# w_out's sums and low halves on GpSimd, x's copies on ScalarE, conversion stages asked for engine by engine

## The chip, the cores and the metric

One core of one Trainium2 chip. The time is that of one execution on the device, in microseconds (us). The five engines each work through their own instructions in order: TensorE (PE in the profile; PEld its weight loads), VectorE (DVE), ScalarE (ACT), GpSimd (POOL) and SyncE (SP), which here asks for nearly all DMAs.

## What is computed

```python
scores = scale * x @ state^T;  xread = softmax(scores) @ state          # x: 8 x 8 heads x 512 x 64
scores2 = scale * state @ x^T; sread = softmax(scores2) @ x             # state: 8 x 8 x 32 x 64
x1 = concat([xread, sread], axis=2), heads side by side                 # 8 x 544 rows of 512
a = x1 @ w1; b = x1 @ w2; x2 = ((a * b) @ w3) @ w_out                   # 512 -> 1024 -> 1024 -> 512
a = x2 @ w_a; b = x2 @ w_b; out = (a * b) @ w_out2                      # 512 -> 1536 -> 512
```

The inputs are doubles. The kernel takes them in as pairs of 32-bit words, and multiplies with matrices that are split into a high and a low half: three products (high by high, high by low, low by high) stand for one.

## The kernel before, in words

**Stages.** First, a list of jobs (`run_jobs`) converts w1, w2, w3 and the first w_out, does the attention of blocks 0 and 1 in part and layer 0; it ends at about 150 us. Then come the layers of attention blocks 1 to 6, one after the other, and at last the layer of block 7 interleaved with the small layer of the state rows (`one` and `one_s`): this is the first block, to about 530 us. The second block (`block2`) takes the eight batches in four pairs g = 0 to 3 and runs to the end; in g = 0 it also computes the state rows.

**A layer.** A layer has eight steps f (`step`, called from `block1`). In a step TensorE makes `ap`, ScalarE copies it to `asbp`, TensorE makes `bp`, VectorE multiplies the two into `hfp` (L1188), and `split` makes the high half on ScalarE (L149) and the low half on VectorE (L155). Only then does TensorE accumulate the step before into four PSUM banks (`flush`, L1223). So four of the eight banks hold the layer's sums, and the other four go around among `ap`, `bp` and whatever attention work needs one.

**What is filled in.** `fills1` has two calls in a step: `middle`, after `ap`, and `behind`, after the split. Each places attention work of the following blocks by the tables MIDDLE and BEHIND and then lets the planner place conversion stages. In step 6 x of block b + 2 is transposed by TensorE (its half 0, two banks), and the banks are copied out behind that step by `x_move`; step 7 does the same with half 1. Each even step also splits a piece of p: ScalarE makes `ph`, GpSimd `pl`; the loads of p are asked for three pieces ahead.

**The conversions.** Three `Intake` objects take in weights that are needed later: `sw` (w1 and w2 again, for the state layer), `ab` (w_a and w_b) and `iz` (the second w_out, class `IntakeZ`). A task is a list of stages: two takes on ScalarE, a join on VectorE (`make`, L199), sums and differences of quarters, high halves on ScalarE with low halves on VectorE or GpSimd, and stores to DRAM. `ab`'s even columns have their sums on GpSimd and low halves on VectorE, the odd ones the other way round; `sw`'s columns have low halves on the one or the other. For w_out all sums (L1113) and all low halves were on VectorE. Here and below w_out, without more, is this second one. One of its tasks covers one of six column blocks c: parts `za`, `zb`, `zc`, `zd`, each stored to `z_d` from SP. The first read of `z_d` is in the second half of g = 0 in `block2`.

**The planner.** `now` is a clock that the kernel's writer advances by an estimate of TensorE's work, `through[e]` when engine e (A ScalarE, V VectorE, G GpSimd, D the DMA queues) is expected to be through with what was asked of it, and `charge` adds a stage's cost to it. `Intake.run` asks for a task's next stages as long as none would begin later than `now` plus a horizon (1.5 in the layers for `sw` and `ab`, 2.0 there for `iz`; 1.5 in the state layer, 2.0 in the second block for all), and enough SBUF units are vacant. A stage that follows another is due 0.2, or 0.7 after a stage of several engines, after the end of that one. What is asked for goes into the engines' queues at that place. Nothing of this runs on the chip: it only fixes the order of instructions.

Of the kernel before, what the change touches and what calls it, by code (L numbers as in the profile page):

```python
# [15 lines left out]
ALU = mybir.AluOpType  # L16
# [42 lines left out]
SW_FROM = 46  # L59
LAG = 0.7  # L60
HORIZON = (1.5, 1.5, 2.0)
START_BY = 3.0
MARGIN = 1.5

# [8 lines left out]
def attention_moe_moe2(  # L73
# [17 lines left out]
    nc = tc.nc  # L91
    B, H, S, D = x.shape
# [24 lines left out]
    now = [0.0]  # L117
    through = {"A": 2.0, "V": 4.0, "G": 3.0, "D": 0.0}
# [21 lines left out]
    def room(n, by=None):  # L140
        return sum(by is None or t <= by for t, _ in vacant) >= n
# [265 lines left out]
    class Attention:  # L407
# [16 lines left out]

        def x_move(self, g):
            self.x_part(g, 0, "A")
            self.x_part(g, 1, "V")

        def x_part(self, g, j, e):
            (nc.scalar.copy if e == "A" else nc.vector.tensor_copy)(self.xt[g][:, j, :], self.banks.pop((g, j)))  # L430
# [153 lines left out]

    PE_COST = dict(x_transpose=0.9, scores=0.9, read=0.9, col_transpose=0.9)
    COST = dict(
        x_move=dict(A=0.6, V=0.7),
        scores_move=dict(A=0.7),
        maxima=dict(V=2.2),
        col_exp=dict(A=1.3),  # L590
# [3 lines left out]
        sums=dict(V=1.5),  # L594
# [268 lines left out]
    for n_early, name in enumerate(EARLY):  # L863
# [10 lines left out]
        elif name[:2] == "w3":  # L874
# [3 lines left out]
            for k in range(2):  # L878
# [13 lines left out]
                    need=2 - 2 * k,  # L892
# [65 lines left out]
    class Intake:  # L958
# [23 lines left out]
        def stages(self, f, raws):  # L982

            o = {}
            name = f"{self.name}{f}"
            eng = "GV"[f % 2]

            def take(i):
                if i == 0:
                    o["c"] = Convert(name, raws[:2])  # L990
                o["c"].take(i)

            def split_columns():
                hi, lo = unit(f"{name}h", F32R), unit(f"{name}l", F32R)
                split(hi, lo, o["c"].out, {"G": nc.gpsimd, "V": nc.vector}[eng])
                free(name)
                self.cols[f] = [v.rearrange("p (w k c) -> p w k c", k=4, w=2) for v in (hi, lo)]

            def halves(t):
                return t.rearrange("p (b c) -> p b c", b=4)  # L1000

            def sums():
                a11, a12, a21, a22 = (halves(o["c"].out)[:, i] for i in range(4))
                o["s"] = unit(f"{name}s")
                s1, s2, s3, s4 = (halves(o["s"])[:, i] for i in range(4))
                e = {"G": nc.gpsimd, "V": nc.vector}[eng]
                for out, x, y, op in (
                    (s1, a21, a22, ALU.add),
                    (s3, a11, a21, ALU.subtract),
                    (s2, s1, a11, ALU.subtract),  # L1010
                    (s4, a12, s2, ALU.subtract),
                ):
                    e.tensor_tensor(out=out, in0=x, in1=y, op=op)

            def split_part(i):
                src, part = ((o["c"].out, name), (o["s"], f"{name}s"))[i]
                hi, lo = (unit(f"w0_{f}_{2 * i + j}", F32R) for j in range(2))
                split(hi, lo, src, {"G": nc.gpsimd, "V": nc.vector}["VG"["GV".index(eng)]])
                free(part)
                o["p", i] = hi, lo  # L1020

            def store_part(i):
                for j, t in enumerate(o["p", i]):
                    for n in range(2):
                        a, b = PLACES[4 * i + 2 * n : 4 * i + 2 * n + 2]
                        nc.sync.dma_start(
                            out=w_d[f][:, a : b + 1 : b - a, j, :].bitcast(F32),
                            in_=t.rearrange("p (h b c) -> p h b c", h=2, b=2)[:, n].bitcast(F32),
                        )
                if f in AB_AT:  # L1030
                    free(*(f"w0_{f}_{2 * i + j}" for j in range(2)), at=until[0] + 2.5)
                else:
                    for m, t in enumerate(o["p", i]):
                        v = t.rearrange("p (b k c) -> p b k c", b=4, k=2)
                        for n in range(4):
                            w_t.setdefault((0, f, 4 * i + n), []).append(v[:, n])
                self.cols[f] = i == 1

            out = [
                (0, dict(A=1.1), lambda: take(0)),  # L1040
                (0, dict(A=1.1), lambda: take(1)),
                (1, dict(V=1.2), lambda: o["c"].make()),
            ]
            if self.plain:
                out.append((2, {"A": 1.1, eng: {"G": 2.4, "V": 1.1}[eng]}, split_columns))
            else:
                other = "VG"["GV".index(eng)]
                work = {"A": 1.1, other: {"G": 2.4, "V": 1.1}[other]}
                out += [
                    (1, {eng: {"G": 2.6, "V": 1.4}[eng]}, sums),  # L1050
                    (2, work, lambda: split_part(0)),
                    (0, dict(D=3.0), lambda: store_part(0)),
                    (2, work, lambda: split_part(1)),
                    (0, dict(D=3.0), lambda: store_part(1)),
                ]
            return deque(out)

        def run(self, horizon, force=False):
            for t in list(self.tasks):
                ready, stages = t  # L1060
                while stages:
                    need, work, go = stages[0]
                    begin = max(t[0], *(through[e] for e in work))
                    if not force and begin > now[0] + horizon:
                        break
                    if not room(need, None if force else now[0] + horizon + 1):
                        break
                    stages.popleft()
                    until[0] = t[0] = charge(**work) + (LAG if len(work) > 1 else 0.2)
                    go()  # L1070
                    until[0] = None
                if not stages:
                    self.tasks.remove(t)
# [13 lines left out]
    class IntakeZ(Intake):  # L1087
# [12 lines left out]
        def stages(self, c, raws):  # L1100
            o = {}

            def take(i):
                if i == 0:
                    o["c"] = Convert(f"z{c}", raws)
                o["c"].take(i)

            def sums():
                b11, b12, b21, b22 = (o["c"].out[:, i * 256 : (i + 1) * 256] for i in range(4))
                o["s"] = unit(f"zs{c}")  # L1110
                t2, t1, t3, t4 = (o["s"][:, i * 256 : (i + 1) * 256] for i in range(4))
                for out, x, y in ((t1, b12, b11), (t2, b22, t1), (t3, b22, b12), (t4, b21, t2)):
                    nc.vector.tensor_tensor(out=out, in0=x, in1=y, op=ALU.subtract)  # L1113

            def parts(name, src, terms):
                t = unit(name, F32R)
                v = t.rearrange("p (i q e) -> p i q e", i=2, q=2)
                src = src.rearrange("p (i e) -> p i e", e=256)
                n = len(terms)
                if n == 2 and src.shape[1] == 4:  # L1120
                    src = src[:, 0:4:2]
                split(v[:, :n, 0, :], v[:, :n, 1, :], src)
                for i, p in enumerate(terms):
                    nc.sync.dma_start(out=z_d[p][:, c].bitcast(F32), in_=v[:, i].bitcast(F32))
                free(name, at=until[0] + 3.0)

            def first():
                parts(f"za{c}", o["c"].out, (0, 1))

            def second():  # L1130
                parts(f"zb{c}", o["s"][:, :512], (2, 3))

            def third():
                parts(f"zc{c}", o["c"].out[:, 768:], (5,))
                free(f"z{c}")

            def fourth():
                parts(f"zd{c}", o["s"][:, 512:], (4, 6))
                free(f"zs{c}")
                self.cols[c] = True  # L1140

            work = dict(A=0.7, V=0.8, D=0.8)
            return deque(
                [
                    (0, dict(A=1.1), lambda: take(0)),
                    (0, dict(A=1.1), lambda: take(1)),
                    (1, dict(V=1.2), lambda: o["c"].make()),
                    (1, work, first),
                    (1, dict(V=1.6), sums),
                    (1, work, second),  # L1150
                    (1, work, third),
                    (1, work, fourth),
                ]
            )

    w_t = {}
    iz = IntakeZ("z", None, False, list(range(NF2 // 2)))
# [267 lines left out]
    for b, qs in ((0, range(4)), (1, range(3))):  # L1425
        for q in qs:
# [5 lines left out]
                need=1,  # L1432
# [83 lines left out]
    for b in range(B):  # L1516
# [9 lines left out]
        def fills1(f, b=b):  # L1526
            def middle():
                attend(MIDDLE, b, f)
                sw.run(HORIZON[0])
                ab.run(HORIZON[0])  # L1530
                iz.run(HORIZON[2])

            def behind():
                if f % 2 == 0:
# [24 lines left out]
                    ab.start(2, reserve=AB_RESERVE)  # L1559
                sw.run(HORIZON[0])  # L1560
                ab.run(HORIZON[0])
                iz.run(HORIZON[2])

            return middle, behind

# [446 lines left out]
```

## Time and profile before

| | us |
|---|---|
| runs, lowest / median / highest of 3 | 1313.37 / 1313.78 / 1316.99 |
| the profiled execution | 1314.6 |
| its span, first to last instruction | 1312.8 |
| TensorE busy | 1281.2 (98%) |
| VectorE busy | 735.3 (56%) |
| ScalarE busy | 569.6 (43%) |
| GpSimd busy | 497.6 (38%) |

The profile is of one execution. TensorE's busy time is a union of its matmuls' times, whose ends are modelled. A wait is idle time of an engine ahead of an instruction, put down to the engine that released it last.

### The profile page before, as it was taken

What the parts mean: (1) busy time and instruction counts of PE and PEld (TensorE: products, weight loads), DVE (VectorE), ACT (ScalarE), POOL (GpSimd) and SP (SyncE); (2) the same over time, 40 slices, a digit from 0 to 9 for tenths busy, and PEclk for the clock granted to TensorE, in tenths of its full rate; (3) what the DMA queues carried; (4) which work ended last, traced back from release to release, by engine and by line L of the source; (5) the groups of instructions that cost most, each with busy time, mean ns of one, the idle gap of its engine ahead of it and who ended that gap; (6) DMA issues with size and microseconds to landing.
All of it is one profiled execution on the core that took longest, in us unless ns stands there. A gap on an engine that the chain in (4) does not pass through costs nothing. (4 is left out here: it accounts for less than half of the span.)

```text
span 1312.8 us, 19793 instructions
## 1 busy us (share of the span) xinstructions
PE 1281.2 (98%) x7642; PEld 1082.0 (82%) x7642; DVE 735.3 (56%) x867; ACT 569.6 (43%) x932; POOL 497.6 (38%) x328
## 2 busy tenths in 40 slices
PE   7999999999999998999999999999999999999998
PEld 5666677877777887988889998889988889988898
DVE  6884145756665666565456862247922369433493
ACT  6876355655565665545233431123511235212232
POOL 3823124525334263345228341148311274212450
PEclk7999999999999999999999999999999999999999
DMA  9968765474556742789564769317695247873271
GB/s 328 346 191 263 230 213 192 129 240 134 199 182 193 237 167 70 264 283 306 196 226 144 248 238 389 127 27 250 203 404 200 64 162 263 331 275 107 81 256 65
DMA packets 129789, 276.55 MB, mean 211 GB/s; under 512 B 13600, under 2 KB 66848, under 8 KB 129696
## 3 DMA queue, kind: packets, MB, share of 16 engines
q1 hardware_dynamic: 125408, 260.09, 58.2%
q0 software_dynamic: 4288, 15.21, 2.9%
q8 instruction: 60, 0.98, 0.3%
q14 instruction: 33, 0.27, 0.1%
HBM read 205.00 MB, written 70.25 MB: 210 GB/s over the span
## 5 line engine op out<-in xcount | busy, mean ns | idle before, releaser
L1807 POOL TENSOR_TENSOR r<-e,e 128x512 f32<-128x512 f32 x48 | 64.2, 1337 | 305.6 <-DVE e L1632 305.6
L1223 PE MATMUL x2p<-hp,ws 128*128 128x512 f32 x672 | 162.2, 390 | 0.3 <-DVE hp L155 0.2
L155 POOL TENSOR_TENSOR pl<-pr,ph 128x512 fp32r<-128x512 f32 x64 | 85.9, 1362 | 174.4 <-ACT ph L149 115.7
L1223 PEld LDWEIGHTS x2p<-hp,ws 128*128 128x128 f32 x672 | 125.7, 188 | 26.9 <-DVE hp L155 0.5
L1752 ACT COPY e<-r 128x512 f32<-128x512 f32 x48 | 28.2, 588 | 190.0 <-PE r L1618 190.0
L1815 DVE TENSOR_TENSOR r<-e,r 128x512 f32<-128x512 f32 x48 | 32.9, 686 | 128.7 <-PE r L1618 128.7
L1188 DVE TENSOR_TENSOR hfp<-asbp,bp 128x512 f32<-128x512 f32 x56 | 38.2, 683 | 79.0 <-PE bp L1164 78.5
L1632 DVE TENSOR_TENSOR e<-e,q 128x512 f32<-128x512 f32 x48 | 32.9, 685 | 73.5 <-PE q L1618 73.3
L1656 POOL TENSOR_TENSOR r<-r,r 128x1024 f32<-128x1024 f32 x24 | 70.6, 2952 | 2.2 <-issue 1.2
L155 DVE TENSOR_TENSOR hp<-hfp,hp 128x512 fp32r<-128x512 f32 x56 | 46.5, 831 | 42.3 <-ACT hp L149 41.6
L1618 PE MATMUL r<-xT2h,w 128*128 128x512 f32 x192 | 67.2, 390 | 0.5 <-ACT e L1752 0.5
L1618 PE MATMUL r<-xT4h,w 128*128 128x512 f32 x192 | 67.1, 390 | 0.2 <-DVE e L1632 0.2
L1618 PE MATMUL r<-xT3h,w 128*128 128x512 f32 x192 | 67.2, 390 | 0.1
L1618 PE MATMUL r<-xB11h,w 128*128 128x512 f32 x192 | 67.0, 390 | 0.0
L1618 PE MATMUL v<-xT1h,w 128*128 128x512 f32 x192 | 66.9, 389 | 0.0
L1618 PE MATMUL q<-xB21h,w 128*128 128x512 f32 x192 | 66.9, 389 | 0.0
L1618 PE MATMUL v<-xB22h,w 128*128 128x512 f32 x192 | 66.9, 389 | 0.0
L149 ACT CAST hp<-hfp 128x512 fp32r<-128x512 f32 x56 | 34.7, 619 | 73.4 <-DVE hfp L1188 70.7
L1780 ACT COPY e<-r 128x512 f32<-128x512 f32 x48 | 28.3, 589 | 69.3 <-PE r L1618 69.3
L1182 ACT COPY asbp<-ap 128x512 f32<-128x512 f32 x56 | 32.8, 586 | 54.4 <-PE ap L1164 54.2
L1632 DVE TENSOR_TENSOR e<-e,v 128x512 f32<-128x512 f32 x48 | 32.8, 684 | 29.9 <-PE v L1618 22.6
L1164 PE MATMUL bp<-ah,ph 128*128 128x512 f32 x112 | 48.0, 429 | 0.0
(499 smaller groups left out, 3731.0 us busy)
## 6 DMA issues: line engine op xcount, KB each, us to landing
w<-w_d SPq DMA_DIRECT2D x132, 512.0 KB, 8.6
zz<-z_d SPq DMA_DIRECT2D x84, 512.0 KB, 4.3
w_d<-w SPq DMA_DIRECT2D x96, 256.0 KB, 5.0
p_d<-sg SPq DMA_DIRECT2D x128, 128.0 KB, 3.2
pr<-p_d SPq DMA_DIRECT2D x32, 512.0 KB, 5.7
w<-w_d SPq DMA_DIRECT2D x36, 256.0 KB, 8.8
x<-in_x_dram SPq DMA_DIRECT2D x16, 512.0 KB, 7.7
sw<-in_moe_w_dram SPq DMA_DIRECT2D x16, 512.0 KB, 5.6
```

The lines of the kernel that those rows point to most:

```text
L149: nc.scalar.copy(hi, src)
L155: (eng or nc.vector).tensor_tensor(out=lo[:, i], in0=src[:, i], in1=hi[:, i].bitcast(F32), op=ALU.subtract)
L1164: nc.tensor.matmul(dst[:, :n], lhsT=l[m], rhs=r[q], start=i == 0 and j == 0, stop=i == k - 1 and j == 2,)
L1182: nc.scalar.copy(a_sb[:, :n], pa[:, :n])
L1188: nc.vector.tensor_tensor(out=hf[:, :n], in0=a_sb[:, :n], in1=pb[:, :n], op=ALU.mult)
L1223: nc.tensor.matmul(acc[j], lhsT=w_s[f][:, m, j * P : (j + 1) * P], rhs=h[:, q, :n], start=per == 1 and f == 0 and i == 0, stop=f == NF1 - ...
L1618: nc.tensor.matmul(t, lhsT=w[m], rhs=xf[g].parts[x][q][:, k, :], start=first and k == 0 and i == 0, stop=k == 1 and i == 2, skip_group_che ...
L1632: nc.vector.tensor_tensor(out=out, in0=x, in1=y, op=ALU.add)
L1656: ENGINES[eng].tensor_tensor(out=out, in0=x, in1=y, op=op)
L1780: nc.scalar.copy(e2, r)
L1807: nc.gpsimd.tensor_tensor(out=h[1], in0=e2, in1=e5, op=ALU.mult)
L1815: nc.vector.tensor_tensor(out=h[0], in0=e1, in1=r, op=ALU.mult)
```

## The change

The edit has four parts. (1) w_out's sums are issued on GpSimd, and its low halves too; the planner's costs for both follow. (2) `x_move` copies both banks of a half on ScalarE for blocks above 2; its cost is 1.2 on ScalarE. (3) The join costs 1.6 in the planner in place of 1.2, for `sw`, `ab` and w_out alike. (4) `Intake.run` may be given a horizon for each engine; `iz.run` in the layers is given 2.0 for ScalarE, 1.5 for VectorE, 3.5 for GpSimd and 4.0 for the DMA queues, in place of 2.0 for all. With a single number the test is the same as before.

```diff
+Z_HORIZON = dict(A=2.0, V=1.5, G=3.5, D=4.0)
...
         def x_move(self, g):
             self.x_part(g, 0, "A")
-            self.x_part(g, 1, "V")
+            self.x_part(g, 1, "A" if self.b > 2 else "V")
...
-        x_move=dict(A=0.6, V=0.7),
+        x_move=dict(A=1.2),
...
-                (1, dict(V=1.2), lambda: o["c"].make()),
+                (1, dict(V=1.6), lambda: o["c"].make()),
...
-                    begin = max(t[0], *(through[e] for e in work))
-                    if not force and begin > now[0] + horizon:
+                    by = horizon if isinstance(horizon, dict) else dict.fromkeys("AVGD", horizon)
+                    late = [max(t[0], through[e]) > now[0] + by[e] for e in work]
+                    if not force and any(late):
                         break
-                    if not room(need, None if force else now[0] + horizon + 1):
+                    if not room(need, None if force else now[0] + by["V"] + 1):
                         break
...
                 for out, x, y in ((t1, b12, b11), (t2, b22, t1), (t3, b22, b12), (t4, b21, t2)):
-                    nc.vector.tensor_tensor(out=out, in0=x, in1=y, op=ALU.subtract)
+                    nc.gpsimd.tensor_tensor(out=out, in0=x, in1=y, op=ALU.subtract)
...
-                split(v[:, :n, 0, :], v[:, :n, 1, :], src)
+                split(v[:, :n, 0, :], v[:, :n, 1, :], src, nc.gpsimd)
...
-            work = dict(A=0.7, V=0.8, D=0.8)
+            work = dict(A=0.7, G=1.4, D=0.8)
...
-                    (1, dict(V=1.2), lambda: o["c"].make()),
+                    (1, dict(V=1.6), lambda: o["c"].make()),
                     (1, work, first),
-                    (1, dict(V=1.6), sums),
+                    (1, dict(G=2.8), sums),
...
-                iz.run(HORIZON[2])
+                iz.run(Z_HORIZON)
```

The last pair of lines stands twice, in `middle` and in `behind` of `fills1`.

## Rows read from the trace of the kernel before

**Rows 1.** The page, part 1: busy us (share of the span) and instructions.

```profile
PE 1281.2 (98%) x7642; PEld 1082.0 (82%) x7642; DVE 735.3 (56%) x867; ACT 569.6 (43%) x932; POOL 497.6 (38%) x328
```

**Rows 2.** The table by stretch: us, busy time of engines (instructions), TensorE's clock, DMA share, GB/s.

```profile
150.00:530.00 380.00, 370.22 (x2317) 297.41 (x2317) 221.32 (x286) 215.74 (x378) 149.04 (x120) 1.00 0.55 179
530.00:700.00 170.00, 169.22 (x921) 146.30 (x920) 88.05 (x148) 72.20 (x126) 62.44 (x44) 1.00 0.70 241
700.00:1313.00 613.00, 605.76 (x3690) 545.78 (x3688) 329.54 (x302) 178.71 (x239) 224.52 (x121) 1.00 0.58 205
```

**Rows 3.** Who waits for whom, TensorE from 150 to 530: us, times, longest.

```profile
PE xt L419 <- DVE xt L430: 4.2, 4, 1.5
PE bs L1164 <- DVE hfp L1188: 2.8, 3, 1.5
PE xt L419 <- DVE hfp L1188: 0.9, 2, 0.5
```

**Rows 4.** TensorE in order of time: start, us, instruction, count [idle before <-releaser].

```profile
209.70 0.63 PE L419 MATMUL xt<-ident,x 128*128 128x128 f32 x4 [0.75 <-DVE xt L430]
...
308.81 0.66 PE L419 MATMUL xt<-ident,x 128*128 128x128 f32 x4 [0.37 <-DVE hfp L1188]
...
310.88 0.63 PE L419 MATMUL xt<-ident,x 128*128 128x128 f32 x4 [1.41 <-DVE xt L430]
...
362.52 0.63 PE L419 MATMUL xt<-ident,x 128*128 128x128 f32 x4 [1.46 <-DVE xt L430]
...
412.55 0.63 PE L419 MATMUL xt<-ident,x 128*128 128x128 f32 x4 [0.59 <-DVE xt L430]
...
500.84 0.39 PE L1164 MATMUL bs<-srh,sw2h 128*128 128x256 f32 x1 [0.50 <-DVE hfp L1188]
...
513.57 0.39 PE L1164 MATMUL bs<-srh,sw3h 128*128 128x256 f32 x1 [1.49 <-DVE hfp L1188]
...
524.39 0.39 PE L1164 MATMUL bs<-srh,sw4h 128*128 128x256 f32 x1 [0.79 <-DVE hfp L1188]
```

**Rows 5.** VectorE and GpSimd in order of time around 308 us.

```profile
303.10 1.25 DVE L199 SCALAR_TENSOR_TENSOR ab<-ab 128x512 uint32<-128x512 uint32 x2
304.35 2.73 POOL L155 TENSOR_TENSOR al<-a,ah 128x512 fp32r<-128x512 f32 x2 [6.80 <-ACT ah L149]
304.39 2.97 DVE L1013 TENSOR_TENSOR ab9s<-ab 128x256 f32<-128x256 f32 x2
307.28 0.41 DVE L1013 TENSOR_TENSOR ab9s<-ab9s,ab 128x256 f32<-128x256 f32 x1
308.07 0.68 DVE L1188 TENSOR_TENSOR hfp<-asbp,bp 128x512 f32<-128x512 f32 x1
```

**Rows 6.** VectorE in order of time, w_out's work at 407 and 511 us.

```profile
407.33 0.38 DVE L1113 TENSOR_TENSOR zs<-z 128x256 f32<-128x256 f32 x1
...
511.63 1.29 DVE L155 TENSOR_TENSOR zc<-z,zc 128x256 fp32r<-128x256 f32 x1 [1.42 <-ACT zc L149]
```

**Rows 7.** Tiles, whole span: durations ns min/median/max, first and last start, shape.

```profile
L1113 DVE TENSOR_TENSOR zs<-z x12: 381/418/1511, 268.1 to 667.8; 128x256 f32<-128x256 f32 x12
...
L1013 POOL TENSOR_TENSOR ab10s<-ab x2: 737/897/1057, 350.2 to 351.2; 128x256 f32<-128x256 f32 x2
...
L1688 SPq DMA_DIRECT2D zz<-z_d x84: 319/320/1436, 699.9 to 1276.5; - x84
L1124 SPq DMA_DIRECT2D z_d<-zd x12: 320/423/705, 350.7 to 673.4; - x12
```

**Rows 8.** Groups of instructions: busy us, mean ns | idle before.

```profile
L155 POOL TENSOR_TENSOR pl<-pr,ph 128x512 fp32r<-128x512 f32 x64 | 85.9, 1362 | 174.4 <-ACT ph L149 115.7 <-DMA p_d<-sg 29.1 <-issue 28.4
```

**Rows 9.** The page, DMA issues: count, KB each, median us to landing.

```profile
pr<-p_d SPq DMA_DIRECT2D x32, 512.0 KB, 5.7
```

**Rows 10.** X's two copies behind step 6, VectorE and ScalarE in order of time.

```profile
208.87 0.68 DVE L430 COPY xt<-xt 128x512 f32<-128x512 f32 x1
...
209.08 0.57 ACT L430 COPY xt<-xt 128x512 f32<-128x512 f32 x1
```

More of the change, by code (lines that the diff above doesn't have):

```diff
@@ L1561, in behind @@
                 ab.run(HORIZON[0])
-                iz.run(HORIZON[2])
+                iz.run(Z_HORIZON)
             return middle, behind
```

## The prediction, made before the change was run

> **What bounds the kernel now.** I read the page's busy times first. TensorE is busy for 1281.2 us of the 1312.8 us span [rows 1], so an edit that leaves its matmuls alone can win no more than the rest, 31.6 us, and only where TensorE waits for an engine that the edit relieves. Next the table by stretch [rows 2]: from 150 to 530 us (the attention layers and the short state layer) TensorE lacks 380 - 370.2 = 9.8 us; from 530 to 700 only 0.8 us; from 700 to the end 7.2 us. The granted clock is 1.00 in all three, so no change of clock is at stake. Before 150 us nothing is edited: the first conversion of the planner starts later, and the job list there keeps its own costs and order. So the 9.8 us are what can be won or lost, 0.7% of the span, and more can be lost than won.
>
> The third view is who waits for whom [rows 3]. Three rows carry most of the 9.8 us: TensorE's x transposes wait 4.2 us in 4 places for VectorE's copy of an earlier x transpose out of PSUM, 0.9 us in 2 places for VectorE's product `hfp` (both give back a PSUM bank), and the state layer waits 2.8 us in 3 places for `hfp`. Then the single waits [rows 4]. All x waits stand in step 7 of a layer, where x's second half needs banks that the first half, copied behind step 6, still holds. In the fourth view, the engines in order of time around 308 us, the reader sees why: VectorE works in order, and ahead of `hfp` it has a join (1.25 us) and the sums of w_a and w_b (2.97 us for two of four) [rows 5]. In other places it is w_out's work: four sums from 407.33 us, and at 511.63 us a low half that sat 1.42 us for ScalarE and then took 1.29 us, right ahead of the `hfp` for which TensorE waits 1.49 us [rows 6]. VectorE is busy 58% of this stretch (221.3 of 380 us) and GpSimd 39% (149.0) [rows 2]; on average there is room on both, so it is a matter of order, not of throughput.
>
> **The change part by part.** The sum is made against the profiled execution, 1314.6 us with its 1312.8 us of span; the median of the runs, 1313.78 us, is 0.8 us less, and the difference is carried to the median.
>
> *w_out's sums and low halves to GpSimd.* Per column block four sums and four low halves leave VectorE, with the waits for ScalarE's high halves. One sum took 0.42 us on VectorE at the median; on GpSimd the same shape takes 0.74 to 1.06 us [rows 7], and half of a 128x1024 low half, the nearest row to a 128x512 one, 1.36 us [rows 8]. So a block costs GpSimd about 4 x 0.9 + 3 x 1.36 + 0.7 (the short one taken as half) = 8.4 us, six blocks 50 us. That lies beside other work: GpSimd is free for 231 us of the 380. Behind the moved instructions in GpSimd's order stand the low halves of p (`pl`) and of the attention (`al`); the sums can run as soon as their join is done, mostly ahead of ScalarE's `ph`, so I take nothing for them, with an upper bound of one set of sums, 3.6 us, ahead of one `pl`. The stores of the parts stay on SP behind their low halves and now wait for GpSimd; behind them on SP are the loads of p, which are asked for three pieces (six steps) ahead and take 5.7 us [rows 9]; that is the cover. What comes back is the two waits whose queue held w_out's work: 0.59 at 412.55 and 1.49 at 513.57 [rows 4, 6]: **-2.1 us**. The bound on this side is nothing, if another piece takes the place.
>
> *Joins costed 1.6 instead of 1.2.* This changes no instruction, only when the planner asks. After a join the next stage is due at its end plus 0.2. With 1.2 that is 1.4 after now, inside the horizon of 1.5 of the layers; with 1.6 it is 1.8, outside. So a join and what follows it can no longer be asked for in the same call, unless the horizon is 2.0 as in the second block. Three of the waits are such pairs: join and sums before 308 us (0.37 + 1.41), join and `sw5l` before 500.84 (0.50), join and low half before 524.39 (0.79) [rows 4, 5]: 3.07 us in all. But the second piece is only put half a step or a step later, ahead of another `hfp`. Bounds: -3.1 and 0; I take half, **-1.5 us**, since a delayed `hfp` in other steps shows no wait in these rows, while the state layer has few steps without one.
>
> *x's second copy from VectorE to ScalarE.* `x_move` runs only for attention blocks 3 to 7, all above 2, so every one of its copies is on ScalarE; VectorE gives up ten copies of 0.68 us. ScalarE's order behind step 6 is high half, `ph`, then x. At 209 us VectorE's copy ended at 208.87 + 0.68 = 209.55 and ScalarE's at 209.65 [rows 10]. The second copy on ScalarE must follow the first and takes 0.57 again, less a little overlap, so I estimate its end near 210.15, 0.6 us later than on VectorE, and the bank with it. The pattern is the same at 310 and 361 us. So where the wait stays (209.70 and 362.52, where the queue ahead of `hfp` holds w_a's and w_b's low halves, which the edit leaves on VectorE) it grows by 0.6 each: **+1.2 us**. Ends: +3.0 if all five layers pay, and -2.2 if these two waits vanish with VectorE's relief (0.75 + 1.46) [rows 4]. What queues behind the added copy on ScalarE is step 7's copy of `ap`, 0.5 us later; it is needed by `hfp` only after the `bp` matmuls, which hides it.
>
> *Asking engine by engine.* A w_out stage is now asked for when GpSimd is up to 3.5 and the DMA queues up to 4.0 late, with ScalarE still at 2.0. The blocks end sooner: today their last parts are stored between 350.7 and 673.4 us [rows 7], while the first read of them comes at 699.9. So nothing waits for their end, and being earlier is worth nothing by itself; but two or three more blocks fall into the layers instead of the second block, each with its takes and high halves on ScalarE and its joins on VectorE. The second block's idle of 0.8 us [rows 2] is all that can be won there. For the layers I take 0, with bounds of 0 and +1.5 (one more wait of the longest kind seen).
>
> Sum: -2.1 - 1.5 + 1.2 = -2.4 us, so 1313.8 - 2.4 = **1311.4 us**.
>
> **The rivals.** (1) *Only rearranged*: each piece that is moved meets another `hfp`, and the waits of 9.8 us keep their sum. For it: four of five step 7s show a wait whatever the piece was (low half, sums of w_a, sums of w_out). Against it: two waits have w_out's work and nothing else ahead of them. Time: 1313.8 us, within 0.6 of it.
> (2) *All of it comes free*: the two stubborn waits vanish as well, since the copy no longer stands behind VectorE's queue: -2.1 - 3.1 - 2.2 = -7.4, so 1306.4 us. Against it: ScalarE's own copy also ended after VectorE's at 209 us, so the queue ahead of `hfp` still decides.
> (3) *GpSimd holds VectorE up*: the two meet in reading SBUF. At 304.39 us two sums on VectorE took 2.97 us together while GpSimd ran `al`, and the next took 0.41 [rows 5]: 1.1 us lost for each meeting. With 50 us more of GpSimd work, and joins, row work and low halves on VectorE ahead of `hfp`, five step 7s that each lose 1.1 us, and +3.0 for the copies, less 2.1 for w_out's own pieces, give +6.4, so 1320.2 us. It decides from three such meetings in step 7 (+4.2). Against it: GpSimd's new pieces come in one call of sixteen per layer, and `hfp` itself reads PSUM and kept 0.68 us. With only two meetings the same working gives +3.1, inside the noise.
> The Trainium skill ("SBUF — State Buffer", section "SBUF: two separate sides") speaks against this change: it says that VectorE with two SBUF inputs and GpSimd share one port pair as an exclusive lock, so that the later of the two is blocked for the other's whole instruction. The 1.52 us against 0.41 us of [rows 5] agree with it. By that rule a meeting would cost up to one GpSimd instruction, 1.36 us in place of 1.1, and rival 3 would come to +7.7.
> (4) *The edit doesn't reach*: were the conversions delayed by a third engine (ScalarE at its unchanged 2.0), the order would hardly change but for the copies, +1.2 to +3.0: 1315 to 1317 us, counted with rival 1 in its chance.
>
> **How the numbers follow.** About 0.3% (3.9 us) is what a measurement of this kernel can tell from no change; the runs before alone spread from 1313.37 to 1316.99. The forecast with its own range of 1308.8 to 1314 us has a chance of 0.52, rivals 1 and 4 together 0.24, rival 2 0.11, rival 3 0.13. The range for eight in ten, 1307.8 to 1317.5 us, reaches into rival 2 and up to rival 3's cheaper half. Faster than 1309.8: rival 2 and the lower quarter of the forecast, 0.11 + 0.14 = 0.25. Slower than 1317.7: most of rival 3, 0.11 and a little of rival 4, together 0.13. The rest, 0.62, is within 0.3%.
>
> **What would show it.** In the changed kernel's trace: no w_out sum or low half on VectorE, and no wait of TensorE like 1.49 at 513.57 or 0.59 at 412.55; no join directly followed by the sums of the same columns in the layers; both copies of an x half end to end on ScalarE, with the waits of the x transposes released by ScalarE and near 1.4 and 2.1 us in layers 1 and 4 (209.70 and 362.52); w_out's last store well before 673.4 us; GpSimd busy for some 50 us more. The prediction is wrong if TensorE's idle from 150 to 530 us is not between 5 and 11 us, if waits appear for `pl` (then GpSimd is the new bound of a step), or if the time moves through the second block, whose matmuls nothing here touches.

## The result, and the profile after

The changed kernel took 1326.76 us at the median of 6 runs (1325.16 to 1328.64), the kernel before 1316.38 us at the median of 6 beside it (1313.37 to 1318.23). The ratio is **1.0083, 95% interval 1.0067 to 1.0100**: slower by some 10.9 us, where 1311.4 us and no measurable change were forecast. The profiled execution took 1328.64 us, with a span of 1326.8 us.

The page's first part answers to [rows 1]. GpSimd has 48.3 us more, VectorE 17.8 us less. (Lines of the changed kernel stand one or two further down than those of the kernel before: its L150 is L149 there.)

```profile
PE 1285.0 (97%) x7642; PEld 1085.4 (82%) x7642; DVE 717.5 (54%) x809; ACT 574.9 (43%) x942; POOL 545.9 (41%) x376
```

The table by stretch answers to [rows 2] (us, busy times with counts, granted clock, DMA share, GB/s). TensorE's idle from 150 to 530 us grew from 9.8 to 13.1 us, from 530 to 700 from 0.8 to 5.5 us, and the clock fell in both; a matmul at half clock counts as busy, so the busy time hides part of the loss.

```profile
150.00:530.00 380.00, 366.86 (x2275) 293.71 (x2274) 209.70 (x248) 221.64 (x394) 182.09 (x153) 0.99 0.59 193
530.00:700.00 170.00, 164.54 (x903) 143.50 (x902) 78.24 (x119) 68.98 (x117) 70.69 (x55) 0.99 0.63 214
700.00:1326.00 626.00, 620.02 (x3764) 558.01 (x3762) 334.95 (x310) 180.88 (x243) 230.81 (x125) 1.00 0.56 201
```

A sharper view is to take the same matmuls in both traces and subtract their starts. TensorE works through the same instructions in the same order in both kernels, so each line below is how far the changed kernel lies behind. Such matmuls are called landmarks from here on:

| TensorE's matmul | before, us | after, us | behind, us |
|---|---|---|---|
| `pb`, ahead of all that is edited | 164.8 | 167.6 | 2.9 |
| `srt`, end of the layers | 462.8 | 464.2 | 1.4 |
| `x2p`, state layer | 481.0 | 490.0 | 9.0 |
| `bs`, state layer | 524.4 | 533.2 | 8.8 |
| `r`, second block | 582.2 | 593.7 | 11.5 |
| `r`, second block | 595.2 | 610.5 | 15.3 |
| `v`, second block | 677.6 | 691.8 | 14.2 |

So the layers gained 1.4 us, one place in the state layer lost 7.6, and one place near 590 us 3.8, with 2.7 lost on the way there and 1.1 won back behind it. Two things cancel between 490.0 and 533.2 us: right behind the 7.6 us the changed kernel fell a further 2.4 us behind (11.5 at its matmul of 496.05), and it got 2.7 back where `bs` no longer waits for `hfp`. Who waits for whom, TensorE from 150 to 530 us, against [rows 3] (total, times, longest):

```profile
PE x2p L1225 <- ACT hp L150: 7.6, 1, 7.6
PE srt L558 <- ACT sn L551: 2.3, 3, 1.4
PE xt L420 <- ACT xt L431: 1.1, 2, 0.8
PE ap L1166 <- POOL pl L156: 0.8, 2, 0.5
```

The waits for VectorE that the prediction was about are gone: 4.2 + 0.9 us of x waits became 1.1, and the state layer no longer waits for `hfp`. In their place stands a single wait of 7.6 us for ScalarE; two waits for `pl`, 0.8 us together, are new. The engines in order of time around it (start, us, engine, line, instruction, [idle before <-releaser]):

```profile
451.96 0.37 SPq L631 DMA_DIRECT2D pr<-p_d  x1
470.58 0.82 SPq L1126 DMA_DIRECT2D z_d<-zd  x2
471.49 1.87 SPq L1318 DMA_DIRECT2D xB<-x_d  x4
473.45 1.22 SPq L954 DMA_DIRECT2D sw<-in_moe_w_dram  x2
474.76 2.57 SPq L165 DMA_DIRECT2D zr<-in_moe_w_out_dram  x2
477.43 0.38 SPq L631 DMA_DIRECT2D pr<-p_d  x1
477.91 10.89 SPq L954 DMA_DIRECT2D sw<-in_moe_w_dram  x4
...
465.46 0.64 ACT L150 CAST zd<-zs 128x512 fp32r<-128x512 f32 x1
...
466.31 2.99 POOL L156 TENSOR_TENSOR sw2l<-sw,sw2h 128x512 fp32r<-128x512 f32 x2
469.27 1.28 POOL L156 TENSOR_TENSOR zd<-zs,zd 128x512 fp32r<-128x512 f32 x1
...
475.97 1.05 ACT L150 CAST sw3h<-sw 128x1024 fp32r<-128x1024 f32 x1
488.29 0.65 ACT L181 ACTIVATE zr<-zr 128x512 f32<-128x512 f32 x1 [11.26 <-DMA zr<-in_moe_w_out_dram]
489.38 0.60 ACT L150 CAST hp<-hfp 128x512 fp32r<-128x512 f32 x1
...
490.04 5.79 PE L1225 MATMUL x2p<-hp,ws 128*128 128x512 f32 x12 [7.63 <-ACT hp L150]
```

SP stood 18.2 us at a store of `zd` whose low half GpSimd made last. GpSimd's part in these 18.2 us is the smaller one: the high half ended on ScalarE only at 466.10, the low half, behind that of `sw2`, at 470.55. Behind the store x (`xB`), two pieces of `sw`, w_out's block 4 (`zr`), p and four more pieces of `sw` went out from 471.49 to 488.80 us. (Before, x's loads went out at 456.77 and block 4 was loaded at 626.67.) The `zr` pieces landed late, ScalarE stood 11.26 us at their take, and the high half of `hfp` was queued behind that take. The table by stretch for 480 to 500 us shows what followed: TensorE ran 2.4 of 10 us while the DMA engines were full, and then at a granted clock of 0.69, a mixture of its two levels (0.50, the lower one, over 490 to 496 us).

```profile
480.00:490.00 10.00, 2.40 (x21) 2.20 (x19) 0.00 (x0) 1.71 (x4) 0.00 (x0) 0.80 1.05 384
490.00:500.00 10.00, 9.96 (x34) 7.60 (x35) 3.44 (x6) 6.24 (x12) 2.50 (x2) 0.69 0.55 175
```

### The profile page after: what moved, and what is told of

Read it like the earlier page. It is cut to its first block, busy times and chain, and to the rows that moved or that the text cites. A ratio compares the mean times of both kernels' runs of the same rounds, so it can differ in the third digit from the quotient of the medians.

```text
span 1326.8 us, 19812 instructions
## 1 busy us (share of the span) xinstructions
PE 1285.0 (97%) x7642; PEld 1085.4 (82%) x7642; DVE 717.5 (54%) x809; ACT 574.9 (43%) x942; POOL 545.9 (41%) x376
## 4 chain that ended last, share of the span: by engine, by line
PE 64%; DVE 4%; ACT 2%; issue 2%; DMA 1%; POOL 0%; DVEq 0%; ACTq 0%; POOLq 0%
PE r L1620 19%; PE ro L1946 10%; PE v L1620 10%; PE vo L1946 5%; PE q L1620 5%; PE x2p L1225 4%; PE abs L1703 3%; PE qo L1946 2%; PE bp L1166 2%; PE ap L1166 2%; DMA zr<-in_moe_w_out_dram 1%; PE srv L1885 1%; DVE r_12l L156 1%; PE x2s L1225 1%; DVE sw L200 0%
## 5 line engine op out<-in xcount | busy, mean ns | idle before, releaser
L1225 PE MATMUL x2p<-hp,ws 128*128 128x512 f32 x672 | 165.0, 395 | 9.1 <-ACT hp L150 7.6
L156 DVE TENSOR_TENSOR hp<-hfp,hp 128x512 fp32r<-128x512 f32 x56 | 53.7, 960 | 63.3 <-ACT hp L150 61.8
L150 ACT CAST hp<-hfp 128x512 fp32r<-128x512 f32 x56 | 34.5, 617 | 42.4 <-DVE hfp L1190 40.7
```

Source lines behind the costliest of these rows:

```text
L150: nc.scalar.copy(hi, src)
L156: (eng or nc.vector).tensor_tensor(out=lo[:, i], in0=src[:, i], in1=hi[:, i].bitcast(F32), op=ALU.subtract)
L1225: nc.tensor.matmul(acc[j], lhsT=w_s[f][:, m, j * P : (j + 1) * P], rhs=h[:, q, :n], start=per == 1 and f == 0 and i == 0, stop=f == NF1 - ...
```

## First experiments: the wait at 490 us

All numbers behind a ratio are 95% intervals. Theory: the loss comes from a w_out load that now stands in a crowded place of SP's queue, behind a store that waits for GpSimd, and from a take that waits in ScalarE's order. Rival: GpSimd's extra work itself.

**hold**: block 4 and 5 are not asked for until the second block.

```diff
-Z_AT = {0: 17, 1: 23, 2: 29, 3: 35, 4: 41, 5: 44}
+Z_AT = {0: 17, 1: 23, 2: 29, 3: 35, 4: 64, 5: 64}
```

> The changed kernel, but w_out's column blocks 4 and 5 are not begun before the second block (step 64 instead of 41 and 44). Theory (late load): in the changed kernel block 4's load falls into a burst of other loads at 471 to 478 us, ScalarE stands 11.3 us at its first take, TensorE 7.6 us at the next accumulation, and some 3 us more go to half clock. Without that load the wait and the half clock vanish: 1326.8 - 9 to 11 = 1316 to 1318 us, no idle of ScalarE over 4 us between 470 and 500 us. Rival (moved work itself: GpSimd and VectorE in each other's way, copies on ScalarE): only the place of two blocks moves, 1324 to 1327 us.

1.0007 [0.9997, 1.0018]: ten of the eleven us are back, with all of the work still on GpSimd. TensorE was busy for 29.17 of the 30 us from 470 to 500 at clock 1.00. SP still stood at the store of `zd` until 468.19, and ScalarE still waited 5.35 us for a piece of `sw`, more than the 4 us expected, but nothing of TensorE's hung on it. The burst itself was as slow as with w_out's block in it: six loads of `sw` landed after 12.1 us at the median (12.0 in the changed kernel). What is gone is w_out's take ahead of the high half of `hfp`.

**pool_stores**: w_out's parts are stored from GpSimd's queue (`nc.gpsimd.dma_start` in place of `nc.sync.dma_start`).

> The changed kernel, but w_out's parts are stored from GpSimd's queue instead of SyncE's. In the changed kernel SyncE stands 18.2 us at the store of block 3's last part, until GpSimd has made its low half, and the loads behind it go out together. Theory (the store's wait on SyncE makes the burst): the loads go out earlier and spread, ScalarE's 11.3 us shrink below 3, 1316 to 1319 us. Rival A (the load is late for its size and its neighbours alone): the wait stays, 1324 to 1327 us. Rival B (GpSimd is the bound): 42 more issues of about 0.55 us each on GpSimd make it 1327 to 1332 us.

1.0028 [1.0012, 1.0044]. SP in order of time; with the same loads in the same order, x's go out 13.7 us and `zr` 7.3 us earlier, and no take of ScalarE waits:

```profile
457.79 5.78 SPq L1318 DMA_DIRECT2D xB<-x_d  x4
463.67 3.66 SPq L954 DMA_DIRECT2D sw<-in_moe_w_dram  x2
467.42 0.93 SPq L165 DMA_DIRECT2D zr<-in_moe_w_out_dram  x2
```

A new wait of 2.17 us for `pl` at 330.44, with a granted clock of 0.83 over 320 to 340 us, took part of the gain back: in GpSimd's order the low half of p now stands behind two stores (1.09 us).

**take_late**: the planner counts block loads as landing 8 us later.

```diff
-self.tasks.append([charge(D=2.9) + 2.0 + MARGIN, self.stages(c, raws)])
+self.tasks.append([charge(D=2.9) + 2.0 + MARGIN + 8.0, self.stages(c, raws)])
```

> The changed kernel, but each w_out task counts its load 8 later, so that its first take is asked for later; the load itself keeps its place in the queue. Theory (late load, in ScalarE's order): the burst of loads stays, but ScalarE meets the take only when the load has landed, so the 11.3 us at ScalarE and TensorE's 7.6 us vanish: 1316 to 1319 us. Rival A (the burst itself holds others up, not the take): 1324 to 1327 us. Rival B (moved work itself): 1324 to 1327 us.

0.9983 [0.9974, 0.9993]. It moved the loads too, not the takes alone (a block is asked for when the last one is done), so it shows that the loss goes with the place, and no more.

**one_horizon**: `iz.run(HORIZON[2])` in both calls, as before; the other three parts stay.

> The changed kernel, but w_out's stages in the layers are asked for with one horizon of 2.0 again, as before the change. Theory (late load): the pace of the blocks changes, so block 4's load falls elsewhere; if it misses the burst, 1315 to 1318 us; if another block's load meets it, near 1326. Rival (moved work itself): all other parts of the change are there, 1324 to 1327 us whatever the pace.

0.9966 [0.9954, 0.9977], the fastest of these four. The rival falls: with the moved work and the copies all there, the kernel is faster than before, and the loss needs the horizons.

**after_d2**: `D=2.0` in `Z_HORIZON` in place of 4.0.

> The changed kernel with the queues' figure of the four horizons back at 2.0 (ScalarE 2.0, VectorE 1.5, GpSimd 3.5 stay). In SP's order one block's loads still stand among the loads of the state layer, behind a store of zd that waits for GpSimd, as in the changed kernel. If any such place makes the load late, TensorE shows a wait of over 3 us with half clock between 470 and 500 and the time is 1321 to 1326. If the changed kernel's loss needs a store that GpSimd finishes late (18.2 us of standing), the stretch is clean when the store here comes earlier, and the time is that of the kernel with one horizon, 1310 to 1315. By the rival that asking for GpSimd 3.5 ahead costs by itself, waits for pl or for GpSimd's pieces show in the layers, and the time is 1316 to 1320 without a late load.

1.0002 [0.9993, 1.0011]: the time was that of the expectation's last case (1316 to 1320 us), but the trace shows the late load of its first, in a milder form. (The profiled execution, 1318.87 us, is one of the slower of twelve, so the others may have waited less.) The burst began at 466.75 (471.49 in the changed kernel), a block of w_out stood in it again, and this time it was a piece of `sw` behind that block for which ScalarE waited (ScalarE and TensorE in order of time):

```profile
490.21 0.65 ACT L181 ACTIVATE sw<-sw 128x512 f32<-128x512 f32 x1 [6.79 <-DMA sw<-in_moe_w_dram]
...
493.04 4.82 PE L1225 MATMUL x2p<-hp,ws 128*128 128x512 f32 x12 [4.19 <-ACT hp L150]
```

So it is not the one tile: in these four traces it takes a late start of the burst and w_out's block in it. Late without it (hold, x's loads at 469.10) costs nearly nothing, early with it (pool_stores, 457.79) little, both cost 4.2 or 7.6 us. Whether the block costs by its loads or by its takes in ScalarE's order was not tried apart; that `sw` lands as late in hold speaks for the takes in the changed kernel, while in after_d2 the piece waited for is one of `sw`.

## Second experiments: one part at a time on the kernel before

**b_gpsimd**: the sums and low halves on GpSimd with costs G=2.8 and G=1.4, nothing else.

> The kernel before with one part of the change: w_out's four sums and four low halves per block on GpSimd, costed at G=2.8 and G=1.4; the one horizon of 2.0, the x copies and the join's cost stay as they were. By the theory (the loss comes from asking engine by engine, not from where the work is done) the waits of 0.59 at 412.55 and 1.49 at 513.57 go, and the loads of block 4 stay behind the state layer as in the kernel before, so the time is 2 us below to 1 us above before, 1314.5 to 1317.5 on a base of 1316.5, with no wait above 3 us between 470 and 500. In every variant so far that has this work on GpSimd the second block from 530 on lost 3.4 to 5 us against before: if that loss belongs to this part it shows here too, with waits of TensorE for the e copies and e adds. By the rival (the moved work itself costs: GpSimd's later low halves hold SP and VectorE up) it is 5 us or more above before, 1321 and up.

0.9966 [0.9956, 0.9976], better than the forecast's -2.1 us: 4.5 us of 1317. Its trace, of the slowest of twelve executions, shows less: the landmarks won 3.4 us from 165 to 524 us and lost 2.3 from there to the end. TensorE's waits from 150 to 530 us:

```profile
PE xt L419 <- DVE xt L430: 2.9, 3, 1.4
PE xt L419 <- DVE hfp L1188: 1.5, 1, 1.5
PE srt L557 <- ACT sn L550: 0.9, 1, 0.9
```

Against [rows 3], the waits of `bs` for `hfp` are all gone, the two that the prediction left to the joins included.

**b_horizon**: the engine-wise horizons alone; the work stays on VectorE.

> The kernel before with one part of the change: w_out's stages asked for engine by engine (ScalarE 2.0, VectorE 1.5, queues 4.0); sums and low halves stay on VectorE. The loads of block 4 then stand in SP's order among the loads that prepare the state layer, as in the changed kernel, but the store ahead of them waits for VectorE, not for GpSimd. By the theory in its narrow form (the load is late because SP stands 18.2 us at a store that waits for GpSimd) SP stands less long here and the time is within 3 us of before, 1314 to 1319. By its wide form (loads of a later block in that burst are late whoever the store waits for, and ScalarE's take of them holds the high half up) TensorE loses 4 to 9 us between 470 and 500 and the time is 1320 to 1326. By the rival that asking engine by engine costs nothing it is 1316 and the 470 to 500 stretch shows no wait over 1 us.

1.0071 [1.0054, 1.0089], but by neither mechanism: 470 to 500 us was clean (30.00 of 30 us). x's loads went out at 473.16 with a block of w_out behind them, but TensorE itself was 6.9 us behind by then, and ScalarE's take of `zr` waited for nothing. VectorE, GpSimd and TensorE in order of time show where the largest piece went:

```profile
519.36 1.52 DVE L1115 TENSOR_TENSOR zs<-z 128x256 f32<-128x256 f32 x1
520.91 1.39 DVE L1115 TENSOR_TENSOR zs<-z,zs 128x256 f32<-128x256 f32 x1
522.23 1.48 DVE L1115 TENSOR_TENSOR zs<-z 128x256 f32<-128x256 f32 x1
523.63 0.41 DVE L1115 TENSOR_TENSOR zs<-z,zs 128x256 f32<-128x256 f32 x1
...
525.10 0.41 DVE L1190 TENSOR_TENSOR hfs<-asbs,bs 128x256 f32<-128x256 f32 x1
...
520.60 2.83 POOL L156 TENSOR_TENSOR sw6l<-sw,sw6h 128x512 fp32r<-128x512 f32 x2
...
525.56 0.50 PE L1166 MATMUL bp<-ah,ph 128*128 128x512 f32 x1 [3.74 <-DVE hfs L1190]
```

Three sums took 1.39 to 1.52 us while GpSimd made low halves, the fourth, after GpSimd was done, 0.41: the slow-down of [rows 5], now ahead of `hfs`. A sum or a join asked for earlier stands ahead of another `hfp` or `hfs`.

**b_xcopies**: both x copies on ScalarE at A=1.2.

> The kernel before with one part of the change: both copies of an x half on ScalarE, costed at A=1.2. The prediction put +1.2 us on this, with ends of -2.2 and +3.0. In the changed kernel the x waits fell from 5.1 to 1.1 us in all; by the theory that this is due to the copies themselves (the copy no longer stands behind VectorE's queue) the x waits fall here too, to 2 us or less, and the time is 1 to 3 us below before, 1313.5 to 1315.5. By the prediction's reading (the queue ahead of hfp decides) the x waits stay between 4 and 8 us and the time is 1316.5 to 1319.5.

0.9993 [0.9982, 1.0003]. The x waits went from 4.2 + 0.9 to 3.7 + 0.9 us, now released by ScalarE: the wait changed its owner and little else. The 0.75 us at 209.70 of [rows 4] became 0.77, not 1.4 (ScalarE and TensorE in order of time):

```profile
209.17 1.07 ACT L430 COPY xt<-xt 128x512 f32<-128x512 f32 x2
...
209.80 0.66 PE L419 MATMUL xt<-ident,x 128*128 128x128 f32 x4 [0.77 <-ACT xt L430]
```

The transposes went on when the first of the two copies had ended, at 209.75, and did not wait for the second, which ended at 210.24.

**b_join16**: joins at V=1.6.

> The kernel before with one part of the change: a join costed 1.6 instead of 1.2, no instruction changed, only the order in which the planner asks. The prediction put -1.5 us on this, with ends of -3.1 and 0, for the pairs of a join and what follows it ahead of hfp: by it the time is 1313.5 to 1316.5 and the waits of 0.37 and 1.41 before 311 us, 0.50 at 500.84 and 0.79 at 524.39 are gone or halved. By the rival (the second piece only meets another hfp) the sum of TensorE's waits for VectorE from 150 to 530 us stays and the time is within 1 us of before; a loss of 2 us or more would show that the order of before was worth something that the rows did not show.

1.0037 [1.0023, 1.0051]: 4.9 us slower, where the forecast had -1.5. From 165 to 514 us it did gain 4.6 us against the landmarks of before. Then the state layer gave back 4.4 us by 534 (two waits of 1.73 and 2.74 us) and 2.7 more by 582, and 582 to 595 us another 3.1. For that last place, ScalarE of the kernel before in order of time:

```profile
575.95 1.05 ACT L149 CAST w<-ab4s 128x1024 fp32r<-128x1024 f32 x1 [2.79 <-POOL ab4s L1013]
580.46 0.68 ACT L180 ACTIVATE ab<-ab 128x512 f32<-128x512 f32 x1 [3.46 <-DMA ab<-in_moe_w_a_dram]
```

And ScalarE, GpSimd, VectorE and TensorE of b_join16:

```profile
580.91 0.68 ACT L180 ACTIVATE ab<-ab 128x512 f32<-128x512 f32 x1 [7.55 <-DMA ab<-in_moe_w_a_dram]
...
584.36 1.06 ACT L149 CAST w<-ab4s 128x1024 fp32r<-128x1024 f32 x1
...
589.11 3.01 POOL L155 TENSOR_TENSOR w<-ab,w 128x512 fp32r<-128x512 f32 x2 [11.45 <-ACT w L149]
...
589.46 1.51 DVE L1013 TENSOR_TENSOR ab5s<-ab5s,ab 128x256 f32<-128x256 f32 x1
591.01 1.40 DVE L1013 TENSOR_TENSOR ab5s<-ab,ab5s 128x256 f32<-128x256 f32 x1
...
594.25 0.50 PE L1618 MATMUL r<-xT4h,w 128*128 128x512 f32 x1 [1.76 <-DVE e L1632]
```

With the join 0.4 dearer, the high half of `ab4s` is asked for after the next column's take instead of before it. The take waits 7.55 us for its load, the high half waits behind it, and joins, sums and low halves then fall together: two sums at 1.4 to 1.5 us beside GpSimd's low half, ahead of the `e` adds that TensorE wants. TensorE lost 1.76 us at 594.25 by this, and 1.52 at 584.03 for ScalarE's copy of `e`, which stands behind the late take. The changed kernel has the same waits for `e`, 1.52 us at 593.68 and 2.46 at 604.59. In all seven kernels here with a join at 1.6 these two waits are 1.2 to 2.0 and 1.8 to 2.8 us, in the nine with 1.2 at most 0.7 and 0.2.

## Third experiments: the parts together

**after_j12**: the changed kernel with the join at V=1.2 (both places).

> The changed kernel with one part undone: a join is costed 1.2 again. In the planned order the loads of w_out's block 4 then stand behind all loads of the state layer, and x's loads no longer stand behind a store of zd. In all seven kernels with a join at 1.6 TensorE was busy for 55.5 to 56.7 of the 60 us from 570 to 630, in all seven with 1.2 for 59.2 to 60.0. If those two are the whole of the changed kernel's loss, there is no wait above 2 us between 470 and 500 here, TensorE is busy for 59 us or more from 570 to 630, and the time is 1308 to 1313 on a base of 1316.5. If asking engine by engine has a price of its own beside the late load (alone, on the kernel before, it cost 1.0071), the time is 1316 or more.

0.9976 [0.9966, 0.9987]. One number of the planner is worth 14 us here. From 570 to 630 us, the table by stretch of the changed kernel and of this one:

```profile
570.00:630.00 60.00, 56.02 (x285) 47.91 (x284) 32.69 (x48) 28.44 (x47) 34.66 (x30) 0.97 0.86 285
```

```profile
570.00:630.00 60.00, 60.00 (x322) 51.90 (x321) 32.66 (x51) 27.99 (x45) 27.83 (x25) 1.00 0.86 293
```

x's loads went out at 458.22, no longer behind a store of `zd`, and TensorE was busy for 29.56 of the 30 us from 470 to 500.

**hold_j12**: hold with the join at V=1.2.

> The changed kernel with the join at 1.2 and w_out's blocks 4 and 5 held back until the second block, as they were in the kernel before. With the join at 1.6 the same hold gave 1.0007 of before, and the landmarks of TensorE lost 4.2 us in the second block. If the join's cost is the cause of that, the loss is 0 to 1.5 us here (GpSimd's work for these two blocks costs some) and the time is 1309 to 1313 on a base of 1316.5; if it comes from the blocks' place or from GpSimd, the time stays within 1.5 us of before.

0.9971 [0.9962, 0.9981], against 1.0007 for hold: TensorE was busy for 59.93 of 60 us from 570 to 630, and its landmarks won 1.2 us between 524 and 666 us; 2.5 were lost behind that.

With the work on GpSimd and the copies on ScalarE in all four:

| ratio to before | join at 1.2 | join at 1.6 |
|---|---|---|
| one horizon | 0.9967 (gpsimd_x) | 0.9966 (one_horizon) |
| engine by engine | 0.9976 (after_j12) | 1.0083 (changed kernel) |

**gpsimd_x**, b_gpsimd and b_xcopies together:

> The kernel before with two parts: w_out's sums and low halves on GpSimd, and both x copies on ScalarE; the join's cost and the one horizon stay. Alone the first part measured 0.9966 of before and the second 0.9993. If the two add up, this is 0.996 or 1311.5 to 1312 on a base of 1317; if the x copies are worth something only once VectorE is relieved (the x waits then go below 2 us) it is 1309 to 1311; if they only trade one wait for another it is 1312 to 1314.

0.9967 [0.9955, 0.9980]: the copies add nothing to b_gpsimd.

**gpsimd_c4**: b_gpsimd, but blocks 4 and 5, which fall into the second block, stay on VectorE (`nc.gpsimd if c < 4 else nc.vector`, costs likewise).

> The kernel before with w_out's sums and low halves on GpSimd for the blocks 0 to 3 alone, which fall into the layers; the last two blocks, loaded from 620 us on beside the second block's w_a and w_b, keep them on VectorE. In every variant with all six blocks on GpSimd the landmarks of TensorE lost 2.7 to 5 us against before from 530 us to the end. If that loss belongs to GpSimd's work of these two blocks, it is gone here and the time is 2 to 3 us below that of the kernel with all six on GpSimd, 1309 to 1310.5 on a base of 1317. If it belongs to the second block being reached earlier (the shared transfer of w_d through SP sets the pace, whatever the engine), it stays and the time is that of the other within 1 us, 1311.5 to 1313.5.

**0.9942 [0.9930, 0.9955]**, 1309.64 us: the lowest time of all, 0.6% below the kernel before. In b_gpsimd and gpsimd_x TensorE waited 1.7 and 2.0 us near 676 us for w_a's and w_b's parts from `w_d`, whose loads stand on SP behind w_out's stores; here it waited 0.5, and the landmarks won 0.1 us from 524 us to the end where those two lost 2.3. From 150 to 530 us its idle is 5.4 us:

```profile
150.00:530.00 380.00, 374.59 (x2345) 302.89 (x2344) 218.58 (x263) 218.29 (x381) 174.75 (x143) 1.00 0.55 182
```

**gx_c4**, the same with the x copies:

> Both of the above: blocks 0 to 3 of w_out on GpSimd, the last two on VectorE, both x copies on ScalarE, one horizon, the join at 1.2. Meant as a version that beats both kernels: if all parts add up, 1308 to 1310 on a base of 1317 (0.993 to 0.995); if the second block's loss stays, 1311 to 1313.

0.9954 [0.9941, 0.9968], 1311.48 us; the intervals overlap, and no gain from the copies shows.

## Why the prediction was wrong, point by point

*What bounds the kernel*: right. The 9.8 us were the stake, and gpsimd_c4 won 4.4 of them in that stretch. But "no change of clock is at stake" held only for the kernel before: a wait of 7.6 us is followed by a slow clock, and 12 matmuls of `x2p` took 5.79 us instead of 2.91 (a group of 12 at 485.95 us of one_horizon).

*w_out's work to GpSimd, -2.1 us*: right in mechanism, too small: 4.5 us alone. In its trace the idle from 150 to 530 us fell by 4.4 us, and all three waits of `bs` for `hfp` went, of which the prediction had one; but a wait for `w_d` took 1.7 us back near 676 us, so the trace does not account for the whole 4.5. GpSimd's 50 us came as 48.3. The sentence on the cover was the incomplete one. It named the loads of p behind w_out's stores on SP, and p indeed cost nothing; x, `sw` and w_out itself stood there too and were not counted.

*Joins at 1.6, -1.5 us (ends -3.1 and 0)*: **failed**. The number was weighed against the three pairs of the layers and the state layer alone, though it moves every stage behind every join to the end of the second block. The gain in the layers came (4.6 us by 514 us in b_join16), and more was lost behind them. Alone it cost 4.9 us, in the changed kernel 14, beside one horizon nothing.

*x's second copy, +1.2 us (ends -2.2 and +3.0)*: inside its ends, but the step behind the +1.2 **failed**. Two waits were to grow by 0.6 us each because the second copy ends later; in b_xcopies they measured 0.77 and 1.47 us against 0.75 and 1.46, for the transposes went on with the end of the first copy. Alone the part gave -0.9 us, with an interval that holds 0. The reading behind it (the queue ahead of `hfp` decides) agrees with b_xcopies, where the waits stayed: on ScalarE the copies stand behind the high half of `hfp`. The 1.1 us of the changed kernel do not come from the copies alone; one_horizon has 0.8, gpsimd_x without the join's cost 3.0 + 1.5.

*Asking engine by engine, 0 (ends 0 and +1.5)*: **failed**, and the largest miss: +9.3 us alone and some 15 in the changed kernel (against one_horizon); beside the join at 1.2 it was +1.2, with overlapping intervals. "Being earlier is worth nothing by itself" was right, and was taken for "costs nothing". Earlier stages bring earlier loads of the next block, and these joined the burst that feeds the state layer. The prediction looked for what queues behind the moved instructions on VectorE and GpSimd, and not for ScalarE's order, where a take that waits for a load holds back a high half that TensorE needs. Of the landmarks' loss of 11.4 us, 7.6 fell on this one wait and 2.4 on the slow clock behind it.

*The sum* added the parts. Measured one by one they are -4.5, +4.9, -0.9 and +9.3 us, together +8.8 beside the 10.9 of the whole, but that is chance: the 9.3 come with w_out's work in VectorE's queue (after_j12, with that work on GpSimd, has no such loss), and of the four kernels in the table above only the one with horizons and dearer join shows the loss.

*Rivals*: the one on the slower side (GpSimd holds VectorE up) gave 1320.2 by a mechanism that is real, 1.4 to 1.5 us for a sum of 0.41, but it did not make the moved work a loss: b_gpsimd is faster. In b_horizon it struck where VectorE's work was moved in time. The changed kernel paid for it once more, 1.49 us of TensorE's time, behind a low half of `hfp` that took 2.71 us beside GpSimd (0.70 at the median; VectorE, GpSimd and TensorE in order of time):

```profile
543.50 2.71 DVE L156 TENSOR_TENSOR hp<-hfp,hp 128x512 fp32r<-128x512 f32 x1 [0.73 <-ACT hp L150]
...
541.51 1.82 POOL L156 TENSOR_TENSOR zd<-zs,zd 128x512 fp32r<-128x512 f32 x1 [2.84 <-ACT zd L150]
543.29 2.37 POOL L1329 TENSOR_TENSOR xB<-xB,xB 128x1024 f32<-128x1024 f32 x1
...
546.27 2.79 PE L1225 MATMUL x2p<-hp,ws 128*128 128x512 f32 x11 [1.49 <-DVE hp L156]
```

The Trainium skill's rule ("SBUF — State Buffer", section "SBUF: two separate sides") was cited for it; these rows and those of b_horizon agree with an exclusive lock. None of the rivals was a late load.

*What was to be seen*: the last store at 639.7 us, no w_out work on VectorE, both copies end to end on ScalarE (211.95, 1.07 us for two), the waits of 0.59 and 1.49 gone, as written. Not as written: the x waits near 1.4 and 2.1 us measured 0.76 and 0.38, and one of three joins is still followed by its sums (228.95). All three signs of error it named came: idle of 13.1 us from 150 to 530, waits for `pl` (only 0.8 us), and time lost through the second block.

*Left open*: why the planner's dearer join puts block 4 among the state layer's loads was read from the order of instructions, not tried step by step. The 2.7 us between 524 and 582 us of the changed kernel are the 1.49 us at 546.27 and the wait for ScalarE's `e`, 1.52 us where the kernel before had 0.45, within 0.1 us.

## What to carry to other kernels

When an edit lets work be asked for earlier, list what follows it on every queue: its loads, what lands behind them, and each in-order engine that takes them in; a take whose load is late stops everything behind it. A planner's cost is an edit of every place that it orders, so it is weighed over the whole span or tried alone. Move parts one by one: here the best kernel keeps one part of the four, and for four of six blocks only.

## What the runs showed that was not expected

Here a wait cost more than its length. After 7.63 us of idle the next 12 `x2p` matmuls took 5.79 us, after 4.19 us of idle 4.82, at full clock 2.91; the granted clock was 0.69 over 490 to 500 us.

The profiles differ ahead of anything edited here. The matmul at 164.8 us of the kernel before came between 0.6 us earlier and 4.3 us later in the others, as wide as most of the differences that were sought. Landmarks compared from there on leave that out, where two spans do not. They still tell of one execution: after_d2 lost 4.3 us by them and 0.3 by its runs, b_gpsimd won 1.2 and 4.5.

With the DMA engines full, a load of 512 KB of `sw` from SP took 12.0 us at the median from 465 to 500 us of the changed kernel, and 4.0 us in one_horizon, where x's loads went out at 446.98 and w_out's at 439.69.
